# A mixture-of-experts kernel: second tiles of 32 rows, an unsplit first product for the pairs, and low parts on VectorE alone

## The chip, the cores and the metric

The kernel runs on one core of one Trainium2 chip. The metric is the device time of one execution in microseconds. TensorE (PE in the profile) multiplies matrices, VectorE (DVE), ScalarE (ACT) and GpSimd (POOL) work element by element, and SyncE (SP) issues transfers. Each engine takes its instructions in the order of its own queue.

## The reference

Three stages stand one behind the other, all in float32.

- Attention: q, k and v of shape (4, 8, 576, 64), with a causal window of 32 positions for half of the heads and a window of 128 with every fourth position for the others. Its output is a table x of 2304 rows by 512.
- Layer 1: of the rows with `x @ w_skip > 0`, each goes to the one of 8 experts with the largest `x @ w_gate`:

```python
h = np.maximum(xc[mask] @ w1[e], 0.0)
y[mask] = gate_w[mask, None] * (h @ w2[e])
```

  with w1 of 512 x 1024 and w2 of 1024 x 512; the result is added to x. Other rows stay as they are.
- Layer 2: each row goes to the two best of 8 other experts by noisy logits, and the two results are added up with their softmax weights.

With the inputs of the runs the experts of layer 1 get 199, 144, 133, 121, 112, 88, 82 and 66 rows; each expert of layer 2 gets 549 to 591.

## The kernel before, in words

**Stages.** Attention runs until about 131 us, layer 1 until about 308, layer 2 until 750, and the last results are scattered to memory by 766.7.

**Layer 1** sorts its experts by their number of rows: rank 0 has the most. It has 11 tiles of up to 128 rows, t = 0 to 10. Ranks 0, 1 and 2 have two tiles each, the others one; the order of ranks is 0, 3, 1, 4, 5, 2, 6, 7. What a tile can't hold would be worked off in a loop at the end, whose number of passes is counted from the data (`much`, L1471) and is 0 here.

A plain tile (`ExpertTile`) has its rows gathered by an indirect transfer, transposed on TensorE (op `x:t` of the list `steps`), multiplied by w1 (`h0:t` and `h1:t`, 16 matmuls of 128 x 128 each at L746, fp32, which the trace records as 32), sent through a ReLU on ScalarE (`ht`, L749), multiplied by w2 (`p0:t` and `p1:t`, L755, 4 fp32 matmuls of 512 columns each, 8 records) and closed on VectorE (`finish`: `xg`, L1355). The second tiles of ranks 1 and 2 aren't handled alone: tiles 3 and 4, and 7 and 8, are pairs (`ExpertPair`), which share each weight. A pair works with numbers split into two parts: ScalarE rounds a number to a high part (`whi`, `xg`, `xh`; `split`, L433), VectorE or GpSimd subtracts it from the number for the low part (`wlo`, `xl`; L434), and `mm3` (L439 to L441) multiplies high by high, low by high and high by low: three matmuls in the fast form for one fp32 matmul. The first product has eight steps `H0` to `H7` of 256 columns with two banks in PSUM; each bank comes free when VectorE has made `xl` (L788) from it. The second product (`P:3` for the first tile, `P:4` for the second) has 24 matmuls of 512 columns per tile.

**Weights.** An expert's weights are four pieces of 1 MB, two of w1 and two of w2 (class `Pieces`). A slot has two halves, `whi` and `wlo`, of 1 MB each. An unsplit piece is loaded into a half as it is; a piece to be split is loaded into one of three `wraw` buffers and cut into a whole slot by four `whi` on ScalarE and four `wlo`. There are five slots in turn, so a slot is filled again when the work on the fifth before it is done. In layer 1 the pairs' four pieces per rank are split, which makes 20 slots; in layer 2 all pieces are split. `every1` and `every2` say which of the low parts go to GpSimd: one in 8 for the pairs, and one in 2, 4 or 8, or all, by expert in layer 2.

**Order.** TensorE's order is written out by hand: the list `steps` for layer 1, loops for layer 2 (`hidden2` with four PSUM banks, `product2`). The orders of the other engines are made by a scheduler from dependencies and priorities. SyncE issues the weights (L482), the rows written back (L1357) and the zeros for the output (`zt`, L1360) in one queue. Between the expert steps, TensorE and VectorE make layer 2's routing: `r`, `l`, `m` make logits (`x2T`, `lgs`; L1193, L1208, L1213), `X` and `Y` steps fill tables with one-hot products (`eqf`, `onehot`, `bvf`, L358 to L388).

Of the kernel before, what the change touches and what calls it, by code (L numbers as in the profile page):

```python
# [8 lines left out]
F32 = mybir.dt.float32  # L9
# [421 lines left out]
def split(nc, hi, lo, src, eng=None):  # L431
# [12 lines left out]
class Pieces:  # L444
# [24 lines left out]
    def load(self, n):  # L469
        while self.loaded < min(n, len(self.keys), self.known):  # L470
            key = self.keys[self.loaded]
            src, every = self.src[key]
            if every is None:
# [49 lines left out]
def tile_attention_moe_moe(ctx, tc, q, k, v, w_skip, w_gate, w1, w2, v_gate, v_noise, noise, u1, u2, out):  # L523
# [17 lines left out]
    ORDER = [c for r in (0, 3, 1, 4, 5, 2, 6, 7) for c in ([K1 + r, r] if r < K1 else [K1 + r])]  # L541
    LAST = 2
# [154 lines left out]

    every1 = {1: 8, 2: 8}
    every2 = [2, 2, 8, 2, 2, 4, 2, 1]
    P = Pieces(tc, raw_p)  # L700
    for kk, src in order:
        P.plan(kk, src, every1.get(kk[1]))
    for e in range(E):
        for i in range(4):

            P.plan((2, e, i), lambda e=e, i=i: piece(u1, u2, e, i, f"o ({'p k' if e > 1 else 'k p'}) f -> p (o k) f"), every2[e])
# [58 lines left out]
    class ExpertPair:  # L765


        def __init__(self, xp):
            x = [xp.tile([128, 2, 256], F32R, name="xg2", bufs=4) for _ in range(4)]
            self.x = x[:2], x[2:]  # L770
            self.h = [xp.tile([128, KC, CAP], F32R, name=n).rearrange("p c t -> p (c t)")[:, :2048].rearrange(
                "p (f t) -> p f t", f=8) for n in ("xh2", "xl2")]

        def rows_T(self, xg, i):
            ps = bank("tp")
            for c in range(KC):
                nc.tensor.transpose(ps[:, 128 * c:128 * c + 128], xg[:, 128 * c:128 * c + 128], ident)
# [397 lines left out]
    static1 = rt.tile([128, E], F32, name="static1")  # L1175
    static2 = rt.tile([128, E], F32, name="static2")
# [45 lines left out]
    with ExitStack() as lctx:  # L1222
# [78 lines left out]
        with ExitStack() as ectx:  # L1301
# [90 lines left out]
            for op, *t in steps:  # L1392
# [70 lines left out]
        def rest_of():  # L1463
# [4 lines left out]
            nc.vector.tensor_scalar(static1, rank1, float(K1), 1.0, op0=ALU.is_lt, op1=ALU.add)  # L1468
            n1 = ro.beyond(wk, cnt1, static1, "1")[1]
# [105 lines left out]
    with tc.If(rest > 0), ExitStack() as ectx:  # L1575
# [34 lines left out]
        xcol1, xe1 = ro.extras(ep, ro.beyond(ep, cnt1, static1, "4"), static1, JR, "4")  # L1610
        rest1 = nc.values_load(much[0:1, 0:1], min_val=0, max_val=JR)
        with tc.For_i(0, rest1, 1) as i:
# [4 lines left out]
            nc.vector.tensor_add(sv[:, 1:2], sv[:, 1:2], so[:, 4:5])  # L1617
            gi = ep.tile([128, 1], I32, name="gir")
# [85 lines left out]
```

## Time and profile before

| | |
|---|---|
| median of 3 runs | 768.95 us (767.02, 768.95, 769.21) |
| profiled execution | 768.6 us, its span 766.7 us |
| TensorE busy | 734.3 us, 96% |
| weight loads of TensorE | 626.3 us, 82% |
| VectorE busy | 379.8 us, 50% |
| ScalarE busy | 309.2 us, 40% |
| GpSimd busy | 245.9 us, 32% |
| low parts on VectorE | 100 operations, 80.8 us |
| low parts on GpSimd | 60 operations, 86.5 us |
| high parts on ScalarE | 160 operations, 91.2 us |

The shares are means over stages that differ: a share of 96% says that TensorE sets the pace over most of the span, and not where the other 4% are. For that the span is read stage by stage, and each hole of TensorE is followed to what ended it. A record of a matmul lasts longer than the distance to the next one, since matmuls are pipelined; for sums the distance counts.

### The profile page before, as it was taken

To read this page: it belongs to the slowest core of one execution; us is meant where nothing else is said; L and a number is where in the kernel's file an instruction comes from. 1 tells how busy PE (TensorE), PEld (TensorE's weight loads), DVE (VectorE), ACT (ScalarE), POOL (GpSimd) and SP (SyncE) were. 2 spreads that over 40 slices of the span, in tenths; PEclk is the share of its full clock that TensorE was granted. 3 is DMA by queue.
4 is the path that set the end of the run, shared out by engine and by line. 5 is a ranking of instruction groups with operands and counts; after the bars stand their busy time and mean duration, and the time that the engine had idled before them with its cause. 6 is when DMAs were issued, how large, how long until landed. Compare 5 with 4: busy or idle time off the path is not lost.

```text
span 766.7 us, 14489 instructions
## 1 busy us (share of the span) xinstructions
PE 734.3 (96%) x5448; PEld 626.3 (82%) x5448; DVE 379.8 (50%) x1253; ACT 309.2 (40%) x824; POOL 245.9 (32%) x239
## 2 busy tenths in 40 slices
PE   8999989979999999899999999999999999999994
PEld 6877767757977887789898997997988988988883
DVE  7766866818217538934344353452552562250110
ACT  5987852124116244224442442533433334333110
POOL 4322220200033043155533533624515325445011
PEclk9999999998999999999999999999999999999997
DMA  7989565597869998243888818729529537223112
GB/s 191 175 185 244 130 210 194 192 331 247 293 219 338 336 316 296 73 110 118 218 277 212 236 69 211 203 74 233 174 85 248 155 109 146 87 40 51 15 25 30
DMA packets 129980, 136.06 MB, mean 177 GB/s; under 512 B 44784, under 2 KB 82416, under 8 KB 129904
## 3 DMA queue, kind: packets, MB, share of 16 engines
q1 hardware_dynamic: 118784, 110.90, 46.4%
q0 software_dynamic: 9808, 22.86, 14.8%
q10 hardware_dynamic: 1312, 1.31, 0.5%
q8 instruction: 45, 0.74, 0.4%
q14 instruction: 31, 0.25, 0.1%
HBM read 103.97 MB, written 31.06 MB: 176 GB/s over the span
## 4 chain that ended last, share of the span: by engine, by line
PE 79%; DVE 7%; DMA 6%; ACT 5%; issue 1%; POOL 1%; SPq 0%; POOLq 0%; DVEq 0%; ACTq 0%
PE pt L439 10%; PE pt L441 10%; PE pt L440 10%; PE po L441 5%; PE po L439 5%; PE po L440 5%; PE s L439 5%; PE s L440 5%; PE s L441 5%; PE s L746 5%; DMA wraw<-in_moe_w_dram 3%; ACT sm L182 3%; PE pt L755 3%; PE s L175 2%; DMA wlo<-in_moe_w_dram 2%; PE tp L146 2%
## 5 line engine op out<-in xcount | busy, mean ns | idle before, releaser
L434 DVE TENSOR_TENSOR wlo<-wraw,whi 128x512 fp32r<-128x512 f32 x100 | 80.8, 833 | 103.5 <-ACT whi L433 95.0
L434 POOL TENSOR_TENSOR wlo<-wraw,whi 128x512 fp32r<-128x512 f32 x60 | 86.5, 1517 | 133.6 <-ACT whi L433 117.1
L439 PE MATMUL pt<-whi,hh 128*128 128x512 f32 (+1 forms) x320 | 126.9, 396 | 0.0
L440 PE MATMUL pt<-wlo,hh 128*128 128x512 f32 (+1 forms) x320 | 126.1, 394 | 0.0
L441 PE MATMUL pt<-whi,hl 128*128 128x512 f32 (+1 forms) x320 | 126.0, 394 | 0.0
L433 ACT ACTIVATE whi<-wraw 128x512 fp32r<-128x512 f32 x160 | 91.2, 622 | 59.0 <-PE po L440 17.1
L716 POOL DMA_INDIRECT xg<-xs,gidx x51 | 53.0, 1040 | 157.9 <-PE tp L1192 32.6
L1216 POOL DMA_INDIRECT out_dram<-y,sidx x40 | 62.9, 1572 | 123.5 <-ACT y L1460 119.9
L441 PE MATMUL s<-xh,wlo 128*128 128x256 f32 (+1 forms) x256 | 72.5, 283 | 0.0
L441 PE MATMUL po<-xh,wlo 128*128 128x352 f32 x224 | 72.5, 324 | 0.0
L440 PE MATMUL s<-xl,whi 128*128 128x256 f32 (+1 forms) x256 | 72.4, 283 | 0.0
L439 PE MATMUL po<-xh,whi 128*128 128x352 f32 x224 | 72.4, 323 | 0.0
L439 PE MATMUL s<-xh,whi 128*128 128x256 f32 (+1 forms) x256 | 72.4, 283 | 0.0
L440 PE MATMUL po<-xl,whi 128*128 128x352 f32 x224 | 72.2, 322 | 0.0
L441 PEld LDWEIGHTS pt<-whi,hl 128*128 128x128 f32 (+1 forms) x320 | 58.4, 183 | 15.7
L440 PEld LDWEIGHTS pt<-wlo,hh 128*128 128x128 f32 (+1 forms) x320 | 58.4, 183 | 15.0
L439 PEld LDWEIGHTS pt<-whi,hh 128*128 128x128 f32 (+1 forms) x320 | 58.4, 182 | 14.7
L1445 DVE SCALAR_TENSOR_TENSOR hl<-po,hh 128x352 fp32r<-128x352 f32 x56 | 29.2, 522 | 69.8 <-ACT hh L1444 68.1
L1460 ACT ACTIVATE y<-pt,slots 128x512 f32<-128x512 f32 (+1 forms) x40 | 27.3, 683 | 79.6 <-PE pt L441 59.3
L182 ACT ACTIVATE sm<-sm,nmax 128x96 f32<-128x96 f32 x144 | 51.9, 362 | 16.3 <-DVE nmax L178 16.0
L1445 DVE SCALAR_TENSOR_TENSOR hl<-s,hh 128x256 fp32r<-128x256 f32 (+1 forms) x64 | 27.4, 428 | 58.1 <-ACT hh L1444 54.3
L186 POOL TENSOR_TENSOR sm<-sm,rs 128x480 f32<-128x480 f32 (+1 forms) x32 | 29.1, 911 | 75.4 <-DVE nmax L178 47.6
(409 smaller groups left out, 1459.0 us busy)
## 6 DMA issues: line engine op xcount, KB each, us to landing
wraw<-in_moe_w_dram SPq DMA_DIRECT2D x40, 1024.0 KB
whi<-in_moe_w_dram SPq DMA_DIRECT2D x12, 1024.0 KB
wlo<-in_moe_w_dram SPq DMA_DIRECT2D x12, 1024.0 KB
xq<-xg SPq DMA_DIRECT2D x24, 256.0 KB
xs<-xq SPq DMA_DIRECT2D x96, 64.0 KB
out_dram<-zt SPq DMA_DIRECT2D x46, 128.0 KB
xs<-xr SPq DMA_DIRECT2D x13, 256.0 KB
v<-in_v_dram SPq DMA_DIRECT2D x7, 432.0 KB
```

Of the source, the lines that this page charges most:

```text
L182: nc.scalar.activation(sm[:, n, :], sm[:, n, :], AF.Exp, bias=nmax[:, n:n + 1], scale=-1.0, accum_out=ssum[:, n:n + 1])
L186: nc.gpsimd.tensor_tensor(out=sm[:, n0:n1, :], in0=sm[:, n0:n1, :], in1=rs[:, n0:n1, None].to_broadcast([128, n1 - n0, 96]), op=ALU.mult)
L433: nc.scalar.activation(hi, src, AF.Copy)
L434: (eng or nc.vector).tensor_tensor(out=lo, in0=src, in1=hi.bitcast(F32), op=ALU.subtract)
L439: nc.tensor.matmul(out, lhsT=a[0], rhs=b[0], start=start, stop=False)
L440: nc.tensor.matmul(out, lhsT=a[0], rhs=b[1], start=False, stop=False)
L441: nc.tensor.matmul(out, lhsT=a[1], rhs=b[0], start=False, stop=stop)
L716: gather.last = nc.gpsimd.indirect_dma_start(out=xg, out_offset=None, in_=xs[:n, :], in_offset=bass.IndirectOffsetOnAxis(ap=idx, axis=0))
L746: nc.tensor.matmul(ph[:, 128 * f:128 * f + 128], lhsT=w[:, c, 128 * f:128 * f + 128], rhs=self.x[:, c], start=c == 0, stop=c == KC - 1)
L1216: s = nc.gpsimd.indirect_dma_start(out=out, out_offset=bass.IndirectOffsetOnAxis(ap=idx, axis=0), in_=y, in_offset=None, compute_op=ALU.add)
L1445: d = nc.vector.scalar_tensor_tensor(hl[1][:, f, s_], in0=ph, scalar=0.0, in1=hl[0][:, f, s_].bitcast(F32), op0=ALU.max, op1=ALU.subtract)
L1460: nc.scalar.activation(y[:n], py, AF.Copy, scale=slots2[:n, 2, j:j + 1])
```

## The change

The second tiles of ranks 1 and 2 now hold 32 rows (`PART`, `rows1`), and places for rows beyond are masked (`rko`, `rkr`). A pair's first product takes w1 unsplit, in plain fp32, over 128 + 32 = 160 columns: 4 matmuls for each `H` step. Its x isn't split any more; ScalarE only copies it. The hidden values are still split, and the second product is still `mm3`, with 32 columns of stationary rows for the second tile. Ranks 1 and 2 so have two pieces to be loaded into halves and two to be cut, and layer 1 uses 18 slots. All low parts are made on VectorE, in both layers. Rows that a tile of 32 can't hold go to the loop at the end (`over1`, `part1`, `done1`), which may have up to 20 passes instead of 16.

```diff
 def split(nc, hi, lo, src):

     nc.scalar.activation(hi, src, AF.Copy)
-    (eng or nc.vector).tensor_tensor(out=lo, in0=src, in1=hi.bitcast(F32), op=ALU.subtract)
+    nc.vector.tensor_tensor(out=lo, in0=src, in1=hi.bitcast(F32), op=ALU.subtract)
...
+    PART = [128, 32, 32, 128, 128, 128, 128, 128]
+    rows1 = [PART[r] if c < K1 or r >= K1 else 128 for c, r in enumerate(RANK)]
...
-            eng = self.nc.gpsimd if j % self.src[key][1] == self.src[key][1] - 1 else self.nc.vector
-            split(self.nc, hi[:, j], lo[:, j], self.raw[key][:, j], eng)
+            split(self.nc, hi[:, j], lo[:, j], self.raw[key][:, j])
...
+    rkr = cp.tile([128, T1], F32, name="rkr")
     for c, r in enumerate(RANK):
-        nc.gpsimd.memset(rko[:, c:c + 1], float(r))
+        nc.gpsimd.memset(rko[:, c:c + 1], float(r + 1))
+        nc.gpsimd.memset(rkr[:, c:c + 1], float(rows1[c]))
+    nc.vector.tensor_tensor(out=rkr, in0=ro.pidx.to_broadcast([128, T1]), in1=rkr, op=ALU.is_lt)
+    nc.vector.tensor_mul(rko, rko, rkr)
+    nc.vector.tensor_scalar(rko, rko, -1.0, None, op0=ALU.add)
...
-    every1 = {1: 8, 2: 8}
-    every2 = [2, 2, 8, 2, 2, 4, 2, 1]
+    cut1 = (1, 2)
     P = Pieces(tc, raw_p)
     for kk, src in order:
-        P.plan(kk, src, every1.get(kk[1]))
+        P.plan(kk, src, kk[1] in cut1 and kk[2] > 1)
...
     class ExpertPair:
-        def __init__(self, xp):
-            x = [xp.tile([128, 2, 256], F32R, name="xg2", bufs=4) for _ in range(4)]
-            self.x = x[:2], x[2:]
...
+        def __init__(self, xp, n):
+            self.n, m = (128, n), 128 + n
+            self.x = [xp.tile([128, 2, 256], F32, name="xg2", bufs=4)[:, :, :m] for _ in range(2)]
...
             for h in range(2):
-                split(nc, *[x[h][:, :, 128 * i:128 * i + 128] for x in self.x], ps[:, h])
+                nc.scalar.activation(self.x[h][:, :, 128 * i:128 * i + n], ps[:, h, :, :n], AF.Copy)
...
-            ph = bank("s")[:, :256]
+            ph = bank("s")[:, :sum(self.n)]
             fs = slice(128 * (f % 4), 128 * (f % 4) + 128)
             for c in range(KC):
-                mm3(nc, ph, (w[0][:, c, fs], w[1][:, c, fs]), [x[c // 2][:, c % 2] for x in self.x], c == 0, c == KC - 1)
+                nc.tensor.matmul(ph, lhsT=w[:, c, fs], rhs=self.x[c // 2][:, c % 2], start=c == 0, stop=c == KC - 1)
...
         def product(self, i, w):
-            py = bank("pt")
+            n = self.n[i]
+            py = bank("pt")[:n]
             for f in range(8):
                 wf = w(f // 4)
-                mm3(nc, py, [h[:, f, 128 * i:128 * i + 128] for h in self.h], (wf[0][:, f % 4], wf[1][:, f % 4]),
+                mm3(nc, py, [h[:, f, 128 * i:128 * i + n] for h in self.h], (wf[0][:, f % 4], wf[1][:, f % 4]),
                     f == 0, f == 7)
...
-    JR, J2 = 16, 48
+    JR, J2 = 20, 48
...
-            nc.vector.tensor_scalar(static1, rank1, float(K1), 1.0, op0=ALU.is_lt, op1=ALU.add)
-            n1 = ro.beyond(wk, cnt1, static1, "1")[1]
+            for to, by in ((static1, [(r < K1) + n // 128 for r, n in enumerate(PART)]), (part1, [n % 128 for n in PART])):
+                nc.vector.memset(to, float(by[0]))
+                for r in range(1, E):
+                    if by[r] != by[r - 1]:
+                        nc.vector.tensor_scalar(over1, rank1, float(r), float(by[r] - by[r - 1]), op0=ALU.is_ge, op1=ALU.mult)
+                        nc.vector.tensor_add(to, to, over1)
+            nc.vector.scalar_tensor_tensor(over1, in0=static1, scalar=128.0, in1=part1, op0=ALU.mult, op1=ALU.add)
+            nc.vector.tensor_tensor(out=over1, in0=over1, in1=cnt1, op=ALU.is_lt)
+            nc.vector.tensor_mul(over1, over1, cnt1)
+            n1 = ro.beyond(wk, over1, static1, "1")[1]
```

On ScalarE, around the end of tile 2's first half (`ht` of the tile in `h0:2`, `lgs` of tile 0's logits), the queue stands before so; `whi` x4 is the cut of a quarter of a piece four times, and `xg` the copies of the pair's transposed rows:

```order
104 L1208 ACTIVATE x2T<-po_2977 128x128
105 L433 ACTIVATE whi<-wraw 128x512 x4
106 L749 ACTIVATE ht_2965<-s 128x512
107 L1213 ACTIVATE lgs<-po_3041 128x16
108 L433 ACTIVATE whi<-wraw 128x512
109 L433 ACTIVATE xg_3073<-tp 128x2x128
110 L433 ACTIVATE whi<-wraw 128x512 x3
111 L433 ACTIVATE xg_3074<-tp 128x2x128
112 L749 ACTIVATE ht_2965<-s 128x512
113 L433 ACTIVATE xg_3073<-tp 128x2x128
114 L1193 ACTIVATE x2T<-tp 128x512
```

and after:

```order
104 L1215 ACTIVATE x2T<-po_2994 128x128
105 L753 ACTIVATE ht_2982<-s 128x512
106 L1220 ACTIVATE lgs<-po_3043 128x16
107 L784 ACTIVATE xg_3075<-tp 128x2x128
108 L784 ACTIVATE xg_3076<-tp 128x2x128
109 L753 ACTIVATE ht_2982<-s 128x512
110 L784 ACTIVATE xg_3075<-tp 128x2x32
111 L784 ACTIVATE xg_3076<-tp 128x2x32
112 L1200 ACTIVATE x2T<-tp 128x512
113 L433 ACTIVATE whi<-wraw 128x512 x4
114 L1215 ACTIVATE x2T<-po_3159 128x128
115 L433 ACTIVATE whi<-wraw 128x512 x4
116 L791 ACTIVATE xh_3077<-s 128x160 x3
```

The eight `whi` around `ht` and `lgs` are no longer there, and of the sixteen for rank 1 the eight for w2 stand ahead of the first `xh`.

On VectorE, ahead of the first `xl` of the pair (`L1355`, after `L1362`, closes tile 2), the queue before:

```order
700 L370 TENSOR_SCALAR onehot<-r_rowsb,ent_lo 128x128
701 L434 TENSOR_TENSOR wlo<-wraw,whi 128x512 x4
702 L362 TENSOR_TENSOR bvf<-eqf,ent_val 128x600
703 L370 TENSOR_SCALAR onehot<-r_rowsb,ent_lo 128x128 x2
704 L358 TENSOR_TENSOR eqf<-pat_2739,ent_col 128x120 x2
705 L314 COPY ohsy<-nextx 128x8
706 L434 TENSOR_TENSOR wlo<-wraw,whi 128x512 x4
707 L1355 SCALAR_TENSOR_TENSOR xg_2793<-pt,slots_2713,xg_2793 128x512
708 L788 SCALAR_TENSOR_TENSOR xl_3078<-s,xh_3077 128x256 x5
```

and after:

```order
707 L358 TENSOR_TENSOR eqf<-pat_2754,ent_col 128x120
708 L1330 TENSOR_TENSOR nextx<-cx,cntx 128x8
709 L358 TENSOR_TENSOR eqf<-pat_2754,ent_col 128x120
710 L314 COPY ohsy<-nextx 128x8
711 L434 TENSOR_TENSOR wlo<-wraw,whi 128x512 x8
712 L1362 SCALAR_TENSOR_TENSOR xg_2810<-pt,slots_2728,xg_2810 128x512
713 L792 SCALAR_TENSOR_TENSOR xl_3078<-s,xh_3077 128x160 x5
```

Two cuts of four stand among the table steps before; now eight stand in one row, right ahead of `xg` and `xl`.

On TensorE, where the pair's first product begins (`H0`), before:

```order
503 L755 MATMUL pt<-wlo,ht_2965 128x512 x4
504 L439 MATMUL s<-xg_3073,whi 128x256
505 L440 MATMUL s<-xg_3075,whi 128x256
506 L441 MATMUL s<-xg_3073,wlo 128x256
507 L439 MATMUL s<-xg_3073,whi 128x256
508 L440 MATMUL s<-xg_3075,whi 128x256
509 L441 MATMUL s<-xg_3073,wlo 128x256
510 L439 MATMUL s<-xg_3074,whi 128x256
```

and after, twelve matmuls of 256 columns have become four of 160:

```order
503 L759 MATMUL pt<-wlo,ht_2982 128x512 x4
504 L790 MATMUL s<-xg_3075,whi 128x160 x2
505 L790 MATMUL s<-xg_3076,whi 128x160 x2
506 L790 MATMUL s<-xg_3075,whi 128x160 x2
507 L790 MATMUL s<-xg_3076,whi 128x160 x2
508 L790 MATMUL s<-xg_3075,whi 128x160 x2
509 L790 MATMUL s<-xg_3076,whi 128x160 x2
```

The names without a split carry `whi` because an unsplit piece lies in a half of a slot.

## Rows read from the trace of the kernel before

**Rows 1.** Windows: start:end, length, busy PE, PEld, DVE, ACT, POOL; clock, DMA share, GB/s

```profile
170.00:180.00 10.00, 7.68 (x47) 7.31 (x47) 8.18 (x27) 5.51 (x14) 0.00 (x0) 0.66 0.95 323
310.00:320.00 10.00, 9.45 (x82) 8.86 (x80) 10.00 (x37) 3.13 (x9) 1.74 (x1) 1.00 0.07 27
320.00:330.00 10.00, 8.22 (x54) 6.66 (x53) 7.91 (x49) 1.28 (x4) 0.00 (x0) 1.00 0.35 107
400.00:500.00 100.00, 100.00 (x559) 88.14 (x558) 45.80 (x66) 40.47 (x79) 44.41 (x35) 1.00 0.68 184
```

**Rows 2.** TensorE's waits, 120 to 330 us: us in total, times, longest

```profile
PE po L324 <- ACT lgs L1213: 4.9, 1, 4.9
PE s L439 <- DVE xl L788: 2.0, 2, 1.1
PE po L324 <- DVE rest0z L382: 1.7, 1, 1.7
```

**Rows 3.** The chain that ended last, 155 to 192 us: start, us, what

```profile
161.30 8.14 DMA wraw<-in_moe_w_dram
...
171.70 0.48 ACT ht L749
...
172.32 0.28 PE po L324
...
187.98 2.50 DVE wlo L434 x4
...
191.53 0.39 PE s L439
```

**Rows 4.** TensorE's instructions in order of time, 160 to 263 us: start, us

```profile
163.58 3.73 PE L746 MATMUL s<-xt,whi 128*128 128x128 f32 x32
...
173.78 5.64 PE L746 MATMUL s<-xt,wlo 128*128 128x128 f32 x32
...
180.21 3.60 PE L755 MATMUL pt<-whi,ht 128*128 128x512 f32 x8
...
187.75 0.28 PE L440 MATMUL s<-xg,whi 128*128 128x256 f32 x1
187.87 0.28 PE L441 MATMUL s<-xg,wlo 128*128 128x256 f32 x1
...
201.94 0.40 PE L439 MATMUL pt<-whi,xh 128*128 128x512 f32 x1
...
261.86 0.41 PE L439 MATMUL pt<-whi,xh 128*128 128x512 f32 x1
```

**Rows 5.** ScalarE's instructions in order of time, 161 to 250 us

```profile
169.51 2.19 ACT L433 ACTIVATE whi<-wraw 128x512 fp32r<-128x512 f32 x4 [8.99 <-DMA wraw<-in_moe_w_dram]
...
184.46 2.18 ACT L433 ACTIVATE whi<-wraw 128x512 fp32r<-128x512 f32 x4
...
247.27 2.20 ACT L433 ACTIVATE whi<-wraw 128x512 fp32r<-128x512 f32 x4 [1.07 <-DMA wraw<-in_moe_w_dram]
```

**Rows 6.** SyncE's queue in order of time, 140 to 310 us

```profile
164.96 7.49 SPq L1360 DMA_DIRECT2D out_dram<-zt  x7
172.73 1.05 SPq L482 DMA_DIRECT2D wraw<-in_moe_w_dram  x2
...
237.86 1.36 SPq L482 DMA_DIRECT2D wraw<-in_moe_w_dram  x2
```

**Rows 7.** VectorE's instructions in order of time, 275 to 325 us

```profile
293.05 1.24 DVE L300 SCALAR_TENSOR_TENSOR iycx<-ent_idle,ixax 128x9 f32<-128x9 f32 x1
...
296.72 0.17 DVE L300 SCALAR_TENSOR_TENSOR iydx<-ent_idle,ixbx 128x9 f32<-128x9 f32 x1
```

**Rows 8.** VectorE's groups by form, 340 to 745 us: busy, mean ns, idle

```profile
L434 DVE TENSOR_TENSOR wlo<-wraw,whi 128x512 fp32r<-128x512 f32 x58 | 51.7, 908 | 85.4 <-ACT whi L433 77.9 <-ACT y L1460 4.2 <-issue 1.6
L1445 DVE SCALAR_TENSOR_TENSOR hl<-po,hh 128x352 fp32r<-128x352 f32 x56 | 29.2, 522 | 69.8 <-ACT hh L1444 68.1 <-issue 1.6
```

**Rows 9.** The page's costliest groups, GpSimd's low parts

```profile
L434 POOL TENSOR_TENSOR wlo<-wraw,whi 128x512 fp32r<-128x512 f32 x60 | 86.5, 1517 | 133.6 <-ACT whi L433 117.1
```

More of the change, by code (lines that the diff above doesn't have):

```diff
@@ L428, in extras, with split @@
         return cols, ei
-def split(nc, hi, lo, src, eng=None):
+def split(nc, hi, lo, src):
     nc.scalar.activation(hi, src, AF.Copy)
-    (eng or nc.vector).tensor_tensor(out=lo, in0=src, in1=hi.bitcast(F32), op=ALU.subtract)
+    nc.vector.tensor_tensor(out=lo, in0=src, in1=hi.bitcast(F32), op=ALU.subtract)
 def mm3(nc, out, a, b, start, stop):
@@ L454, in __init__, with plan @@
         self.known = 4
-    def plan(self, key, src, every):
-        if every is not None:
+    def plan(self, key, src, cut):
+        if cut:
             self.split.append(len(self.keys))
         self.keys.append(key)
-        self.src[key] = (src, every)
+        self.src[key] = (src, cut)
     def slot(self):
@@ L471, in load @@
             key = self.keys[self.loaded]
-            src, every = self.src[key]
-            if every is None:
+            src, cut = self.src[key]
+            if not cut:
                 if not self.half:
@@ L726, in tile_attention_moe_moe, with __init__ @@
     class ExpertTile:
-        def __init__(self, pool, xg):
-            self.pool, self.xg = pool, xg
+        def __init__(self, pool, xg, n=128):
+            self.pool, self.xg, self.n = pool, xg, n
         def rows_T(self):
-            self.x = self.pool.tile([128, KC, 128], F32, name="xt1")
-            self.h = self.pool.tile([128, 8, 128], F32, name="ht1")
+            n = self.n
+            self.x = self.pool.tile([128, KC, 128], F32, name="xt1")[:, :, :n]
+            self.h = self.pool.tile([128, 8, 128], F32, name="ht1")[:, :, :n]
             ps = bank("tp")
             for c in range(KC):
-                nc.tensor.transpose(ps[:, 128 * c:128 * c + 128], self.xg[:, 128 * c:128 * c + 128], ident)
-            nc.scalar.activation(self.x, ps.rearrange("p (c t) -> p c t", c=KC), AF.Copy)
+                nc.tensor.transpose(ps[:, 128 * c:128 * c + n], self.xg[:n, 128 * c:128 * c + 128], ident[:n, :n])
+            nc.scalar.activation(self.x, ps.rearrange("p (c t) -> p c t", c=KC)[:, :, :n], AF.Copy)
         def hidden(self, g, w, f0=0, f1=4):
@@ L1175, in tile_attention_moe_moe @@
     static1 = rt.tile([128, E], F32, name="static1")
+    part1 = rt.tile([128, E], F32, name="part1")
+    over1 = rt.tile([128, E], F32, name="over1")
     static2 = rt.tile([128, E], F32, name="static2")
@@ L1346, in start @@
                     xg = (h1[0], ep, wk, ep)[t % 4].tile([128, DM], F32, name="xg1", bufs=1 + t % 2)
-                    X[t] = ExpertTile((h1[0], ep)[t % 2], gather(xg, gidx1[:, c:c + 1], N))
+                    X[t] = ExpertTile((h1[0], ep)[t % 2], gather(xg, gidx1[:, c:c + 1], N), rows1[c])
                     with tc.issue_after(gather.last.ins):
@@ L1352, in finish @@
             def finish(t):
-                c, x = ORDER[t], X[t]
+                c, x, n = ORDER[t], X[t], X[t].n
                 x.x2 = x.xg
-                nc.vector.scalar_tensor_tensor(x.x2, in0=x.py, scalar=slots[:, 1, c:c + 1] if t else val0[:, 2:3],
-                                               in1=x.xg, op0=ALU.mult, op1=ALU.add)
+                nc.vector.scalar_tensor_tensor(x.x2[:n], in0=x.py, scalar=slots[:n, 1, c:c + 1] if t else val0[:, 2:3],
+                                               in1=x.xg[:n], op0=ALU.mult, op1=ALU.add)
                 d = nc.sync.dma_start(xs[N + 128 * c:N + 128 * c + 128, :], x.x2)
@@ L1400, in tile_attention_moe_moe @@
                     if t in PAIRS:
-                        pair[t] = pair[t + 1] = ExpertPair(xp)
+                        pair[t] = pair[t + 1] = ExpertPair(xp, X[t + 1].n)
                     if t in pair:
@@ L1609, in tile_attention_moe_moe @@
         nc.vector.tensor_copy(ent_val[:, :, :NT, 5:7], ent_val[:, :, :NT, 0:2])
-        xcol1, xe1 = ro.extras(ep, ro.beyond(ep, cnt1, static1, "4"), static1, JR, "4")
+        xcol1, xe1 = ro.extras(ep, ro.beyond(ep, over1, static1, "4"), static1, JR, "4")
+        oe = ep.tile([128, JR, E], F32, name="oe1")
+        ef1 = ep.tile([128, JR], F32, name="ef1")
+        done1 = ep.tile([128, JR], F32, name="done1")
+        nc.vector.tensor_copy(ef1, xe1)
+        nc.vector.tensor_tensor(out=oe, in0=ef1[:, :, None].to_broadcast([128, JR, E]),
+                                in1=ro.eidx[:, None, :].to_broadcast([128, JR, E]), op=ALU.is_equal)
+        first = ep.tile([128, E], F32, name="first1")
+        nc.vector.scalar_tensor_tensor(first, in0=ro.eidx, scalar=32.0, in1=static1, op0=ALU.mult, op1=ALU.add)
+        oe2 = ep.tile([128, JR, E], F32, name="oe2")
+        nc.vector.tensor_mul(oe2, oe, first[:, None, :].to_broadcast([128, JR, E]))
+        nc.vector.tensor_reduce(out=ef1, in_=oe2, axis=AX.X, op=ALU.add)
+        nc.vector.tensor_tensor(out=ef1, in0=ef1, in1=xcol1, op=ALU.is_equal)
+        nc.vector.tensor_mul(oe, oe, part1[:, None, :].to_broadcast([128, JR, E]))
+        nc.vector.tensor_reduce(out=done1, in_=oe, axis=AX.X, op=ALU.add)
+        nc.vector.tensor_mul(done1, done1, ef1)
+        nc.vector.tensor_tensor(out=done1, in0=done1, in1=ro.pidx.to_broadcast([128, JR]), op=ALU.is_le)
         rest1 = nc.values_load(much[0:1, 0:1], min_val=0, max_val=JR)
```

17 lines of the change are left out of this document (9 added, 8 removed).

## The prediction

> **What bounds the kernel now.** I read the table of windows first, for TensorE's share in each stage. In 400–500 us, the middle of layer 2, TensorE is busy 100.00 of 100 us at granted clock 1.00, VectorE only 45.80 [rows 1]: nothing taken off another engine can shorten that stretch. In layer 1 the same table has holes: 170–180 us has 7.68 busy of 10 at a granted clock of 0.66, 320–330 has 8.22, and 310–320 has 9.45 beside a VectorE that is busy 10.00 of 10. The list of waits says what ends the holes [rows 2]: one wait of 4.9 us for ScalarE's `lgs`, two waits of together 2.0 us for VectorE's `xl`, one of 1.7 us for `rest0z`. The chain of waits explains the first [rows 3]: a raw weight transfer takes 8.14 us from 161.30, ScalarE then makes four `whi`, and only behind them, in its queue's order, come `ht` (171.70) and `lgs`, which TensorE waits for until 172.32. The list of ScalarE's instructions has the same [rows 5]: `whi` x4 began at 169.51 after 8.99 us of idling for `wraw`. So the long hole is a queue held by a transfer, not work.
>
> **The change, part by part.** Sums are against the profiled execution, 768.6 us (span 766.7), which lies 0.35 below the median of 768.95.
>
> (a) The wait at 167 us. With rank 1's w1 unsplit there is no cut to make before the pair's w2 pieces, so the eight `whi` in front of and behind `ht` and `lgs` are gone (first order excerpt). `h0:2` ends at about 167.3 (3.73 us from 163.58 [rows 4]); `ht` and `lgs` then follow at once; in the chain TensorE goes on 0.62 after `ht` began (171.70 to 172.32 [rows 3]), and with what `ht` itself waits for I put that near 168.1 instead of 172.3: 4.2 us. The granted clock fell after this hole: `h1:2` has 32 records in 5.64 us from 173.78 where the same form at 163.58 has 3.73 [rows 4], and the transposes ahead of it lost about half a microsecond too. With an idle of 0.75 in place of 4.88 I take the clock to stay: 2.4 us. Bounds for that term: 0 (the clock falls all the same) to 2.6. The last product of tile 2 then ends near 180.6 instead of 187.2.
>
> (b) The pair's first product. Before, each of the 8 `f` takes 12 matmuls of 256 columns, spaced 0.118 (187.75 to 187.87 [rows 4]): 1.41 us. After, 4 fp32 matmuls of 160 columns, two records each in this trace. No row has 160 columns. From the two fp32 forms, after subtracting the 0.16 by which a record outlasts its spacing: 128 columns (3.73 − 0.16)/32 = 0.112, 512 columns (3.60 − 0.16)/8 = 0.43 a record; on the line between them 0.138, so 8 x 0.138 = 1.10 us. Bounds: 0.112 (as 128 columns) to 0.16 (somewhat above the line, as 12 records of the old form by time) a record, 0.90 to 1.28 us. Saved 0.31 per `f`, 2.5 a pair. Transposes of 32 rows save some 0.25 a pair. The second product keeps its 24 matmuls of 512 columns for either tile: nothing.
>
> (c) The wait ahead of `H2`. It stays, in another place. Only the split of rank 1's two w2 pieces is left, and ScalarE has these eight `whi` ahead of the first `xh` (first excerpt), VectorE the eight `wlo` and tile 2's closing `xg` ahead of `xl` (second excerpt); the bank of `H0` comes free with `xl`, and `H2` waits for it. The two raws are issued from 172.73, behind the seven zero transfers that hold SP for 7.49 us [rows 6]; 2 MB at the 323 GB/s of 170–180 us [rows 1] are 6.5 us, so I take them to land near 178 and 181. Then `whi` x4 2.19 [rows 5] to 183.3, the last `wlo` 0.62 (2.50 for four), and 1.05 for `xg` and `xl`, as from 190.48 to 191.53 [rows 3]: `H2` at about 185.1. `H0` and `H1` end at 182.8, so TensorE idles some 2.4 us; before, `H2` stood at 191.5. Gain so far 6.4, rounded to 6.3 for the handing over between engines. Ends: 182.8 (no wait) and 188.5 (raw as late as the `whi` of 184.46 [rows 5], plus the same chain).
> From `H2` to `P:3` before: 201.94 − 191.53 = 10.4, of which 6 x 1.41 matmuls and 1.9 other work; after 6 x 1.10 + 1.9 = 8.5. `P:3` at 193.7: gain 8.2.
>
> (d) The second pair. Before, its raws waited in SP until 237.86 [rows 6], the last `whi` x4 began at 247.27 on a transfer [rows 5], and `H2` waited 1.1 us (second of the two waits in [rows 2]). After, 18 in place of 20 slots are used, w1 needs no cut, and rank 2's w2 pieces take slots that are free two tiles earlier: no transfer is late. Gone: 1.1 wait, 2.5 matmuls, 0.25 transposes. Late next is VectorE's table steps (`bvf`, `onehot`), about 8 us in a stretch of 9 to 10: I take 0.5 back. `P:7` before at 261.86 [rows 4]; gain there 8.2 + 3.85 − 0.5 = 11.5.
>
> (e) The low parts on VectorE. 60 operations leave GpSimd (1517 ns each [rows 9]); VectorE gets them and loses 16 in layer 1, net 44, nearly all of the 60 in layer 2. Price in layer 2: TensorE and its weight loads have no wait there, VectorE is 46% busy [rows 1] and would be some 55%; `hl` at 522 ns [rows 8] has to follow TensorE through four banks, a slack of several microseconds against a burst of four `wlo` (2.5). I take 0; ends 0 and 60 x 0.62 = 37 us, if every one stood in front of an `hl` that TensorE waits for. In the transition (275–325 us) VectorE gets 4 to 10 more `wlo` at 0.62, and loses what GpSimd costs it now: `iycx` took 1.24 beside a GpSimd `wlo`, its like 0.17 alone [rows 7]; I reckon with four or five such excesses of 0.5 to 1.1, about 4 us. Net −2 to +2: I take 0.
> The Trainium skill, "SBUF — State Buffer", section "Who interferes with whom", has a rule for this: a VectorE instruction with two SBUF inputs contends with a GpSimd one that reads SBUF, and the later one blocks wholly. The 1.24 against 0.17 agrees with it.
>
> (f) Small work. Eleven more operations of about 0.17 us [rows 7] stand on VectorE near the first gather; and TensorE, busy with the first rank's tiles, has no wait there that I would lengthen. 0 to 1.9, taken as 0.5 with the memsets at the start.
>
> Sum: 768.6 − 11.5 + 0.5 = 757.6 us.
>
> **The rivals.**
> 1. *The wait only moves to `H2`.* Raws land as late as the `whi` of 184.46 suggests, `H2` at 188.5 and 3.3 of (c) lost: 760.9. For it: SP's queue is unchanged up to these raws. Against it: ScalarE began that `whi` behind another wait, not on the transfer.
> 2. *VectorE becomes the bound of the transition.* It is already at 10.00 of 10 in 310–320 [rows 1]; ten `wlo` more at 0.62, with no contention returned, cost up to 6: 757.6 + 4 to 6 = 762 to 764. Against it: VectorE waits for long stretches before 310.
> The Trainium skill speaks against the change here: "Perfetto Trace Analysis", section "Optimizing Scalar/DVE Operations", holds that work of a saturated VectorE may well be moved to ScalarE or even GpSimd, though between VectorE and GpSimd, which share a port, it might not help. By its first half this rival is right, by its second half my zero; the full 10.00 us agrees with the first, the 1.24 with the second.
> 3. *Slower.* In layer 2 VectorE's one queue holds `hl` behind a `wlo` that waits for its `whi`, and so for a slot or a transfer; on GpSimd that wait hurt nobody. VectorE's `wlo` wait 77.9 us for `whi` in this stretch already [rows 8], hidden. The mechanism decides once a single hold exceeds what the four banks cover, about 5 us; with 1.5 us exposed at each of the 8 x 2 hidden halves it is 24 us, 781. Break-even is at 11 us in all. Against it: the present waits cost TensorE nothing, so they stand in places where no `hl` is due.
> 4. *Only TensorE's own work counts.* Holes at 167 and 191 stay in another form, and 2 x 2.75 us of matmuls and transposes are all: 763.6.
>
> A change that does not do what it says: ranks 1 and 2 have 144 and 133 rows, so 128 + 32 hold them and the loop for the rest runs no pass. I give that no chance.
>
> **How the numbers follow.** Forecast 0.58; rival 1 0.12; rival 2 0.12; rival 4 0.10; rival 3 0.08. A difference under 0.3% (2.3 us: 766.6 to 771.3) can't be told from none here. Faster: all of the forecast and of rivals 1 and 2, and 0.06 of rival 4, whose 763.6 lies 3 us below the bound: 0.88. The same: the other 0.04 of rival 4 and 0.02 of rival 3, near its break-even: 0.06. Slower: the other 0.06 of rival 3. Lowest: no wait at `H2` (−2.4), 0.9 us per `f` (−3.2) or 2 from the transition: 752. Highest: rivals 2 and 4 with a microsecond of small work: 764.5.
>
> **What would show it.** In the profile after: no wait for `lgs` over 1 us near 167 and clock 1.00 in 170–180 (a); 4 fp32 matmuls in 1.10 us (b); a wait of about 2.4 us for `xl` near 183 and `P:3` near 194 (c); `P:7` near 250 (d); TensorE 100 of 100 in 400–700 (e). The forecast is wrong if TensorE shows waits for `hl` in layer 2, or if the 10 us gained by `P:7` are not there at the end.

## The result, and the profile after

The changed kernel takes 760.21 us, the median of 4 runs (758.75 to 761.13), against 768.71 us for the kernel before, timed with it (767.02 to 769.21). The ratio is 0.990, with a 95% interval from 0.9863 to 0.9937. The profiled execution took 760.57 us with a span of 758.8, 7.9 us less than before. The forecast was 757.6, its range 752 to 764.5.

The windows of the changed kernel (start:end, length, busy us of PE, PEld, DVE, ACT, POOL, then granted clock, DMA share and GB/s) answer to [rows 1]:

```profile
170.00:180.00 10.00, 10.00 (x64) 6.74 (x62) 5.97 (x32) 2.57 (x7) 0.95 (x1) 1.00 0.90 312
180.00:190.00 10.00, 7.13 (x43) 5.70 (x42) 6.45 (x12) 4.92 (x14) 0.00 (x0) 1.00 1.05 390
300.00:310.00 10.00, 9.38 (x80) 8.95 (x78) 9.85 (x42) 3.38 (x11) 0.00 (x0) 1.00 0.02 6
310.00:320.00 10.00, 8.22 (x47) 6.90 (x47) 6.99 (x39) 0.77 (x2) 0.00 (x0) 0.83 0.29 105
400.00:700.00 300.00, 300.00 (x1692) 265.91 (x1691) 136.09 (x223) 114.44 (x224) 67.56 (x48) 1.00 0.56 146
```

The stretch 170–180 us, which had 7.68 busy us at a clock of 0.66, is full at 1.00. A new hole stands in 180–190. In 300–320 TensorE's holes and VectorE's full load are those of before, some 10 us earlier, with a lower clock behind them. Layer 2 is at 300 of 300 us.

The list of TensorE's waits (us in total, times, longest), against [rows 2]:

```profile
PE s L790 <- DVE xl L792: 2.9, 1, 2.9
PE po L324 <- DVE ohsz L1134: 2.3, 1, 2.3
PE po L324 <- ACT lgs L1220: 0.6, 1, 0.6
PE tp L726 <- DMA xg<-xs,gidx: 0.5, 1, 0.5
```

The wait for `lgs` has gone from 4.9 to 0.6 us. In place of two short waits for `xl` there is one of 2.9, and the wait in the transition has 2.3 where it had 1.7 and 0.5 in a second one.

TensorE's instructions in order of time (start, us, what), against [rows 4]; the names of lines have moved by a few (L750 is L746, L790 the pair's first product):

```profile
164.67 3.73 PE L750 MATMUL s<-xt,whi 128*128 128x128 f32 x32
...
169.18 0.23 PE L324 MATMUL po<-ohsx,r_tri 128*128 128x144 bf16 x1 [0.65 <-ACT lgs L1220]
...
170.06 3.74 PE L750 MATMUL s<-xt,wlo 128*128 128x128 f32 x32
...
182.01 2.34 PE L790 MATMUL s<-xg,whi 128*128 128x160 f32 x16
187.22 1.35 PE L790 MATMUL s<-xg,whi 128*128 128x160 f32 x8 [2.87 <-DVE xl L792]
...
195.64 0.51 PE L439 MATMUL pt<-whi,xh 128*128 128x512 f32 x1
```

The second `L750` takes 3.74 us, as the first does, where [rows 4] had 5.64. The row of 16 records is `H0` and `H1`, and `H2` at 187.22 carries the wait. `P:7` starts so:

```profile
251.51 0.51 PE L439 MATMUL pt<-whi,xh 128*128 128x512 f32 x1
```

ScalarE's list, against [rows 5], shows `lgs` with nothing of a cut ahead of it, and the two cuts for w2, each begun on the landing of its transfer:

```profile
168.94 0.19 ACT L1220 ACTIVATE lgs<-po 128x16 f32<-128x16 f32 x1
...
179.52 2.19 ACT L433 ACTIVATE whi<-wraw 128x512 fp32r<-128x512 f32 x4 [4.07 <-DMA wraw<-in_moe_w_dram]
...
183.05 2.19 ACT L433 ACTIVATE whi<-wraw 128x512 fp32r<-128x512 f32 x4 [1.18 <-DMA wraw<-in_moe_w_dram]
```

The same two transfers leave SyncE behind seven zero transfers, as in [rows 6]:

```profile
166.05 7.23 SPq L1367 DMA_DIRECT2D out_dram<-zt  x7
173.62 0.99 SPq L481 DMA_DIRECT2D wraw<-in_moe_w_dram  x2
```

Three places that the table below needs and that were not shown of the kernel before: `H0`, the routing of the last two tiles (`ohsz`) and that routing's last matmul.

```profile
187.23 0.68 PE L439 MATMUL s<-xg,whi 128*128 128x256 f32 x1
...
322.13 0.18 PE L324 MATMUL po<-ohsz,r_tri 128*128 128x16 bf16 x1 [1.72 <-DVE rest0z L382]
...
330.47 0.18 PE L333 MATMUL po<-cz,r_ones 128*128 128x8 bf16 x1
```

Where the 7.9 us come from, place by place, worked out from these starts (after: 311.72 and 321.48 for the last two). The last column has the prediction's terms; rounded, they add up to 11.2, where its sum has 11.0.

| from | to | before, us | after, us | gain | forecast |
|---|---|---|---|---|---|
| start | first half of tile 2 (`h0:2`) | 163.58 | 164.67 | −1.1 | −0.5 |
| `h0:2` | routing behind `lgs` | 8.74 | 4.51 | 4.2 | 4.2 |
| that | `H0` | 14.91 | 12.83 | 2.1 | 2.4 |
| `H0` | `H2` | 4.30 | 5.21 | −0.9 | −0.2 |
| `H2` | `P:3` | 10.41 | 8.42 | 2.0 | 1.9 |
| `P:3` | `P:7` | 59.92 | 55.87 | 4.0 | 3.4 |
| `P:7` | routing of the last two tiles | 60.27 | 60.21 | 0.1 | 0 |
| that | its last matmul | 8.34 | 9.76 | −1.4 | 0 |
| that | end of the span | 436.2 | 437.3 | −1.1 | 0 |

### The profile page after: what moved, and what is told of

Its sections match the earlier page's. It is cut to its first block, busy times and chain, and to the rows that moved or that the text cites. A ratio compares the mean times of both kernels' runs of the same rounds, so it can differ in the third digit from the quotient of the medians.

```text
span 758.8 us, 14282 instructions
## 1 busy us (share of the span) xinstructions
PE 728.5 (96%) x5384; PEld 616.8 (81%) x5384; DVE 378.6 (50%) x1302; ACT 299.7 (40%) x808; POOL 162.3 (21%) x190
## 4 chain that ended last, share of the span: by engine, by line
PE 86%; DVE 5%; ACT 4%; DMA 3%; issue 1%; POOL 0%; POOLq 0%; SPq 0%; ACTq 0%; DVEq 0%
PE pt L441 10%; PE pt L440 10%; PE pt L439 10%; PE s L750 6%; PE pt L759 6%; PE po L441 5%; PE po L440 5%; PE po L439 5%; PE s L441 4%; PE s L440 4%; PE s L439 4%; ACT sm L182 3%; PE s L175 3%; PE s L790 2%; PE tp L146 2%; PE pt L197 1%
## 5 line engine op out<-in xcount | busy, mean ns | idle before, releaser
L434 DVE TENSOR_TENSOR wlo<-wraw,whi 128x512 fp32r<-128x512 f32 x144 | 93.4, 685 | 116.7 <-ACT whi L433 101.9
L433 ACT ACTIVATE whi<-wraw 128x512 fp32r<-128x512 f32 x144 | 82.1, 624 | 53.0 <-DMA wraw<-in_moe_w_dram 16.2
L439 PEld LDWEIGHTS s<-xh,whi 128*128 128x128 f32 x256 | 48.7, 190 | 0.7
L440 PEld LDWEIGHTS s<-xl,whi 128*128 128x128 f32 x256 | 48.7, 190 | 0.3
```

Of the source, the lines that this page charges most:

```text
L434: nc.vector.tensor_tensor(out=lo, in0=src, in1=hi.bitcast(F32), op=ALU.subtract)
L439: nc.tensor.matmul(out, lhsT=a[0], rhs=b[0], start=start, stop=False)
L440: nc.tensor.matmul(out, lhsT=a[0], rhs=b[1], start=False, stop=False)
```

## The experiments

Each of these was timed against the kernel before on the same chip: 768.24 us for the first four, 767.35 for the last three. Every trace is of one execution.

**Low parts alone.** One part of the change in the kernel before: no low part of layer 2 on GpSimd. (An 8 in `every2` sends none there, since a piece has only four low parts; so the 8 in `every1` sent none either, and all 60 were layer 2's.)

```diff
-    every2 = [2, 2, 8, 2, 2, 4, 2, 1]
+    every2 = [8] * E
```

> The kernel before with one part of the change alone: all low parts of layer 2 on VectorE, none on GpSimd. My theory (layer 2 is set by TensorE, which has no wait there): 768.7 within 2 us, TensorE 100 of 100 us in 400-700, the hole near 320 within 1.5 us of its 2.3 us before. Rival, VectorE's queue exposes the moved work: 5 to 25 us slower, with waits of TensorE for hl in layer 2. Second rival, contention of GpSimd and VectorE was what cost the transition: 2 to 4 us faster.

768.51 us, ratio 1.001 (0.998 to 1.0039). Its waits from 120 us to the end, and its window of layer 2:

```profile
PE s L439 <- DVE xl L788: 2.5, 2, 1.6
PE po L324 <- DVE ohsz L1129: 2.4, 1, 2.4
PE po L324 <- ACT lgs L1213: 2.3, 1, 2.3
```

```profile
400.00:700.00 300.00, 300.00 (x1683) 264.94 (x1682) 139.22 (x227) 115.00 (x225) 66.43 (x48) 1.00 0.56 147
```

TensorE has no wait in layer 2, though VectorE now makes 108 `wlo` in 340–745 us instead of 58. The moved work costs nothing that can be told from the median, and gains nothing (the interval leaves room for 1.5 us faster to 3 slower): the first theory holds, both rivals fall. The list holds a second lesson: layer 1 is here that of the kernel before, yet the wait for `lgs` is 2.3 us, not 4.9. Its length hangs on when the raw piece lands, and that differs from execution to execution: the first `whi` began at 167.34 here and at 169.51 in the kernel before, though the transfer was issued later here, at 161.83 instead of 161.30. The granted clock fell behind the shorter wait too, to 0.57 in 171–175.

**128 rows.** The changed kernel, with full second tiles:

```diff
-    PART = [128, 32, 32, 128, 128, 128, 128, 128]
+    PART = [128, 128, 128, 128, 128, 128, 128, 128]
```

> The changed kernel, but with 128 rows in the second tiles of ranks 1 and 2, so the pairs' first product takes the unsplit w1 over 256 columns. My theory: the wait for lgs near 168 stays at 0.7 us and the clock at 1.00, which keeps some 6.5 us of the gain; each H step takes 8 records at about 0.22, 1.75 us against 1.09, which costs 16 x 0.66 = 10.5, less up to 1.3 that the wait ahead of H2 gets shorter: 760.2 + 9 = 769, about the time before. Rival, what counts is the wait taken away and the columns hardly at all: 762 to 764.

769.84 us, ratio 1.0025 (1.0001 to 1.005). TensorE's first product of the pair:

```profile
189.63 2.61 PE L790 MATMUL s<-xg,whi 128*128 128x256 f32 x8 [2.42 <-DVE xl L792]
...
195.97 3.62 PE L790 MATMUL s<-xg,wlo 128*128 128x256 f32 x16
```

Two `H` steps (16 records) take 3.62 us, and less the overhang of 0.16 a step is 1.73; the forecast had 1.75. The wait for `lgs` is 0.6 as in the changed kernel, and the clock stays at 1.00 behind it. But it fell behind the wait of 2.42, to 0.61 in 190–194: the 8 records of the first row are one `H` step and take 2.61. From `H2` to `P:3` are 13.9 us, where 6 x 1.73 and the 1.9 of other work make 12.3; 1.6 went to the clock in this execution, which at 772.03 us is 2.2 above its median. So the unsplit w1 by itself wins the waits and loses as much in matmuls: without the narrower tile the change would have been worth nothing.

**w1 split.** The changed kernel, with the pairs' w1 and x split as before, over 160 columns:

```diff
-        P.plan(kk, src, kk[1] in cut1 and kk[2] > 1)
+        P.plan(kk, src, kk[1] in cut1)
...
-                nc.tensor.matmul(ph, lhsT=w[:, c, fs], rhs=self.x[c // 2][:, c % 2], start=c == 0, stop=c == KC - 1)
+                mm3(nc, ph, (w[0][:, c, fs], w[1][:, c, fs]), [x[c // 2][:, c % 2] for x in self.x], c == 0, c == KC - 1)
```

> The changed kernel, but with w1 and x of the pairs split again: 12 fast matmuls of 160 columns for each H step. My theory: the wait for lgs near 168 is back at about 4 to 5 us with the lower clock behind it (some 6.5 us lost), while an H step takes 12 x 0.075 to 0.118 = 0.9 to 1.4 us against 1.09: 762 to 768. Rival, the 32 rows alone make the gain and the unsplit w1 adds nothing: 758 to 761.

768.77 us, ratio 1.0008 (0.9984 to 1.0032): slower than either theory's range had it, by 0.8 us and more. Two matmuls of the first `H` step, and the windows of the second pair:

```profile
186.52 0.28 PE L440 MATMUL s<-xg,whi 128*128 128x160 f32 x1
186.63 0.27 PE L441 MATMUL s<-xg,wlo 128*128 128x160 f32 x1
```

```profile
235.00:245.00 10.00, 9.25 (x45) 4.93 (x44) 7.31 (x20) 5.73 (x14) 5.24 (x5) 1.00 0.92 297
245.00:255.00 10.00, 8.65 (x58) 8.18 (x57) 5.98 (x15) 3.18 (x9) 0.00 (x0) 0.78 1.03 345
255.00:265.00 10.00, 10.00 (x66) 9.91 (x65) 5.17 (x18) 2.45 (x7) 0.94 (x1) 0.70 1.05 392
```

The spacing is 0.11 us, against 0.118 for 256 columns [rows 4]: 96 columns less save 6%, and an `H` step takes 1.33 instead of 1.41. So narrowing the tile gains some 1.3 us in 16 steps as long as w1 is split (an estimate from these spacings). The waits for `lgs` (2.2 us, not the 4 to 5 of my theory) and `xl` (2.3) are back. In this execution the clock also fell behind a hole of 1.35 us at 248.6, to 0.50 in 250.7–260.7, which costs some 5 us (10 us at a spacing of 0.213); the execution took 773.66 us, 4.9 above the median of the 12 runs, so it is not the rule.

The two halves of the change in layer 1 so need each other: either alone (each with all low parts on VectorE) gives about 0, together 8.

**Zeros later.** The changed kernel, with tile 1's seven zero transfers issued behind tile 2:

```diff
-            ZERO = [0, 7, 14, 17, 20, 24, 35, 39, 39, 45, 46, 46]
+            ZERO = [0, 7, 7, 17, 20, 24, 35, 39, 39, 45, 46, 46]
```

> The changed kernel with the seven zero transfers behind tile 1 issued behind tile 2 instead, so that rank 1's two raw pieces of w2 no longer stand behind them in SyncE's queue. My theory (the wait of 2.9 us ahead of H2 comes from the raws' late landing): the wait is under 0.6 us, P:3 starts 2.3 to 2.9 us earlier, and the end is 757.5 to 758.5. Rival, the time is given back later in layer 1 or in the transition, because the zeros or VectorE's steps hold the second pair: P:3 earlier, but 759.5 to 761 in all.

757.17 us, ratio 0.9858 (0.9822 to 0.9894). SyncE's queue and the start of `P:3`:

```profile
165.22 0.34 SPq L1364 DMA_DIRECT2D xs<-xg  x1
165.76 1.44 SPq L481 DMA_DIRECT2D wraw<-in_moe_w_dram  x2
```

```profile
192.09 0.50 PE L439 MATMUL pt<-whi,xh 128*128 128x512 f32 x1
```

The raws leave at 165.8 instead of 173.6, and TensorE has no wait for `xl` at all. Counted from the last matmul of layer 1's first routing (134.24 here, 135.25 in the changed kernel), `P:3` comes 2.5 us sooner; from `P:3` to the end it is 562.8 here and 563.2 there. The time is kept, as the theory had it (the median is 0.3 below its range). The interval overlaps that of the changed kernel, so it is the trace that shows the 2.5 us.

**GpSimd kept.** The changed kernel, with the 60 low parts of layer 2 on GpSimd (the old `every2` and `split`).

```diff
+    every2 = [2, 2, 8, 2, 2, 4, 2, 1]
...
```

> The changed kernel, but with the 60 low parts of layer 2 on GpSimd as before. My theory (where they are made does not matter): within 1.5 us of the changed kernel's 760.2, the hole near 312 us between 1.7 and 2.4 us. Rival, VectorE's moved work made the hole and the lower clock behind it that cost the changed kernel some 2 us after the second pair: 757 to 758.5, hole under 1.2 us. Other rival, contention with GpSimd costs more than the moved work: 762 to 764.

760.2 us, ratio 0.9897 (0.985 to 0.9944), the changed kernel's ratio. Its waits, 120 to 330 us:

```profile
PE s L792 <- DVE xl L794: 3.6, 1, 3.6
PE po L324 <- DVE rest0z L382: 1.6, 1, 1.6
PE po L324 <- ACT lgs L1222: 0.6, 1, 0.6
PE po L388 <- DVE onehot L370: 0.5, 1, 0.5
```

The hole in the transition is 1.6 us and 0.5 in a second wait, together about what it is with all low parts on VectorE, and the clock fell behind it here too (0.80 in 310–315). From `P:7` to the routing's last matmul are 70.1 us here and 70.0 in the changed kernel. So the moved work did not make the hole, nor the lower clock. (The clock also fell behind the 3.6 us ahead of `H2`, to 0.59 in 186–190, which it didn't in the changed kernel.)

**Without the code for the rest.** The changed kernel without the mask on `rko` and all of `over1`, `part1` and `done1`; the code for rows that a tile of 32 can't hold is left out.

```diff
-            for to, by in ((static1, [(r < K1) + n // 128 for r, n in enumerate(PART)]), (part1, [n % 128 for n in PART])):
...
+            nc.vector.tensor_scalar(static1, rank1, float(K1), 1.0, op0=ALU.is_lt, op1=ALU.add)
...
```

> The changed kernel without what it adds for rows that a tile of 32 can't hold: the mask at the start, the eleven small operations near the first gather and the code ahead of the loop are left out (no row needs them with these inputs). My theory: the first tile's steps start 0.7 us earlier and the first gathered rows' transposes 1.1 us earlier, so 759.0 to 759.6. Rival, none of it is on the path: 760.2 within 0.4; the 1.1 us later start then comes from something else.

761.11 us, ratio 0.9916 (0.9883 to 0.995): not faster, and 0.5 above the rival's range too. The last matmul of layer 1's first routing starts at 135.4 here, at 135.3 in the changed kernel, at 132.4 in the execution of "GpSimd kept", which has all that code, at 134.6 in the kernel before and at 136.7 in that of "128 rows". My expectation fell: the later start isn't shown to come from the change, and it differs between executions by up to 4 us.

**Zeros later, and the routing of the last tiles two steps later.** On top of "zeros later":

```diff
-                  (0, 5): [RZ.place, TY.step],
+                  (0, 7): [RZ.place, TY.step],
```

> Like zeros_later, and the routing step of the last two tiles (place of z, with its matmuls at L324) stands behind the last step of expert 0's first hidden half instead of two steps earlier, so that TensorE has two steps of real work while VectorE gets there. My theory (TensorE waits 2.3 us for VectorE's routing at that place, and then loses about 1.3 us to the lower clock): the hole shrinks below 1 us, the clock stays at 1.00, and 2 to 3.5 us are gained on zeros_later's 757.2: 753.7 to 755.2. Rival, the wait only moves to the next step, since VectorE's queue is full there and the hidden steps' banks wait for hl: within 0.7 us of zeros_later.

752.06 us, ratio 0.980 (0.9756 to 0.9844), clear of the changed kernel's interval. TensorE around that routing, and two windows:

```profile
306.09 0.18 PE L324 MATMUL po<-ohsz,r_tri 128*128 128x16 bf16 x1
...
309.61 0.46 PE L388 MATMUL po<-bvf,onehot 128*128 128x280 bf16 x2 [0.46 <-DVE bvf L362]
```

```profile
300.00:305.00 5.00, 5.00 (x44) 4.91 (x43) 4.92 (x28) 1.50 (x5) 0.00 (x0) 1.00 0.00 0
305.00:310.00 5.00, 4.49 (x29) 3.40 (x28) 4.87 (x33) 0.63 (x2) 0.00 (x0) 1.00 0.59 183
```

(A step of the table, `TY.step`, moves along with the routing.) The routing's first matmul finds its input there; of the 2.3 us one wait of 0.46 is left, and the clock stays at 1.00. From `P:7` to that routing's last matmul are 66.9 us here, 69.7 in "zeros later": 2.8 us, within what was expected. The median is 5.1 us lower, 1.6 below the expected range. In the two profiled executions the last matmul of layer 1's first routing starts 1.9 us earlier here (132.38 against 134.24); that such an earlier start is the rest of the medians' difference too isn't shown. This version beats both kernels.

## Why the prediction was right, and where it was off

**(a) The wait at 167 us** was sized to a tenth: 4.2 us and 2.1 of 2.4 for the clock. But that it agrees so closely is in part luck, since both come from one execution of the kernel before. "Low parts alone" and "w1 split", where the cut of rank 1's w1 also stands ahead of `lgs`, show that wait at 2.3 and 2.2 us. From `h0:2` to `H0` they take 20.2 and 20.1 us, the kernel before 23.7 and the changed kernel 17.3: by those two executions the unsplit w1 gains 2.8 us there, by the profile before 6.3. Which of them is usual isn't shown. The execution of "low parts alone" took 766.19 us, 2.3 below the median of its 12 runs, and the profiled one of the kernel before lay 0.35 below its median; the medians of the two kernels differ by 8.5 us, the profiled executions by 8.0.

**(b) The matmuls.** A record of 160 columns takes (2.34 − 0.16)/16 = 0.136 us, 0.138 was interpolated; 1.09 us a step, 1.10 forecast. The second product did not change.

**(c) The wait ahead of `H2`** came in the place and by the chain that the prediction gave: raws behind the zeros, `whi`, eight `wlo`, `xg`, `xl`. Its size was 2.9, not 2.4: the second raw landed at 183.05, two microseconds later than I took it, of which 0.9 is its later issue (173.62, where I reckoned with 172.73). "Zeros later" took the wait away by the queue alone, which shows the cause. The measured 760.21 lies nearer to rival 1's 760.9 than to the forecast, but not by rival 1's mechanism: that had `H2` at 188.5 behind a wait of 5.7 us (from 182.8). `H2` came at 187.22 because `H0` itself stood at 182.01 instead of 180.6, and from `H0` to `H2` only 0.7 us more went than forecast.

**(d) The second pair** gained 4.0 instead of 3.4: the 0.5 that I gave back to VectorE's table steps was not taken.

**(e) The low parts** show no wait of TensorE in 340–745 us, as forecast, and rival 3 is gone: `wlo` has 108 operations there at a mean of 685 ns against 908 in [rows 8]. So VectorE's load hardly grew: 136.09 us of 400–700, or 45%, where I had 55% and the kernel before has 131.28:

```profile
400.00:700.00 300.00, 300.00 (x1679) 264.66 (x1678) 131.28 (x185) 116.44 (x228) 123.84 (x91) 1.00 0.57 150
```

The longer `wlo` come with GpSimd's share: "GpSimd kept" has 928 ns, "low parts alone" 684. The line of the changed kernel:

```profile
L434 DVE TENSOR_TENSOR wlo<-wraw,whi 128x512 fp32r<-128x512 f32 x108 | 70.0, 685 | 94.4 <-ACT whi L433 89.1 <-issue 2.8 <-DMA xs<-xq 1.6
```

In the transition `iycx`, which took 1.24 us beside a GpSimd `wlo` [rows 7], takes 0.16:

```profile
281.01 0.16 DVE L300 SCALAR_TENSOR_TENSOR iycx<-ent_idle,ixax 128x9 f32<-128x9 f32 x1
```

So the contention was real, as the Trainium skill has it ("SBUF — State Buffer", "Who interferes with whom"). Its end pays for the added `wlo` from `P:7` to the routing of the last two tiles: VectorE makes 20 of them there instead of 10 and is busy for the same time, before and after:

```profile
261.86:322.13 60.27, 58.00 (x381) 46.08 (x380) 40.92 (x140) 21.68 (x51) 17.62 (x12) 1.00 0.69 241
251.51:311.72 60.21, 57.87 (x381) 44.55 (x381) 40.90 (x152) 22.26 (x51) 1.94 (x2) 1.00 0.67 238
```

The net of zero was right up to there. Rival 2's mechanism is there, VectorE at 9.85 of 10 in 300–310, but the hole is about what it is with GpSimd's share kept (2.3 against 1.6 and 0.5).

**The step that was mis-sized** is the end of (e): for the transition the sum has 0, with ends of 2 us either way, and no term for the clock. The prediction had named it as a sign of being wrong that the gain by `P:7` is not there at the end; `P:7` came 10.35 us sooner, the end 7.9. So 2.5 us went in between, and in that the account fell short, though the time is within its range. The wait for `ohsz` was followed by a clock of half speed:

```profile
311.72 0.18 PE L324 MATMUL po<-ohsz,r_tri 128*128 128x16 bf16 x1 [2.34 <-DVE ohsz L1134]
...
313.50 0.41 PE L439 MATMUL s<-xh,whi 128*128 128x256 f32 x1
...
314.14 0.41 PE L439 MATMUL s<-xh,whi 128*128 128x256 f32 x1
```

Matmuls of 256 columns stand 0.215 us apart, where [rows 4] has 0.118; that is the lower level, 1.2 GHz, and lasted 2.5 us, some 1.2 of them lost; the table has 1.4 for the stretch. In the kernel before the same hole, 1.7 us behind one of 0.55, had no such tail. Nor had "low parts alone" and "128 rows" behind the same hole of 2.4 and 2.3 us: from that routing to its last matmul they take 8.3 us as the kernel before does, where the changed kernel takes 9.8. "GpSimd kept" has the lower clock, so the 1.4 us can't be put down to the moved work. It fell in five of the six traces of the changed kernel and its variants that have this hole, and in neither of the two others; whether the change has a part in it or an execution's chance, isn't shown.

Up to the transposes of the next gathered rows, which wait 0.45 for their transfer, 0.65 more went. Here the moved work does seem to cost a little. GpSimd issues the first of these gathers, before and after:

```profile
331.26 0.96 POOL L716 DMA_INDIRECT xg<-xs,gidx  x1 [19.52 <-DVE bcnt L1466]
323.13 0.94 POOL L719 DMA_INDIRECT xg<-xs,gidx  x1 [49.61 <-DVE xt L399]
```

That is 0.8 us behind the routing's last matmul before, and 1.65 after, though VectorE's operations in between take the same time. In "GpSimd kept" it is 0.8 as well, in the six other traces, all with no low parts on GpSimd, 1.3 to 1.65; the transposes come 4.3 us behind that matmul in the two with GpSimd's share and 4.6 to 5.1 in the rest. Why GpSimd starts later after its long idling isn't shown. The remaining 0.4 I have not followed. The 0.6 that the start came later than forecast is spread between executions, by "without the code for the rest".

Rival 4, that only TensorE's own work counts, falls with the second row of the table, and with "128 rows": there the `H` steps cost 16 x 0.32 = 5.1 us more than before, and the median is only 1.6 longer (0.1 to 3.8 by the interval). The rest, some 3 us, is waits that went.

## What to carry to other kernels

A wait may be removed by taking work out of the queue ahead of it, but look at once for what stands ahead of the next wait: here the next raws of the same queue held `H2`, and a line that changes the order of issue gave 2.5 us more. Before counting on narrower tiles, find what sets the spacing of the matmuls: with a new weight for every split matmul, 160 columns instead of 256 saved 6% here, and four unsplit matmuls of 160 columns in place of twelve of 256 saved 0.32 us of 1.41. Size a wait from more than one execution: the one at 167 us was 4.9 us in the profile and 2.2 to 2.3 in two other traces with the same cause. And a gain in front of a stage that ends in another engine's hole arrived there whole (60.27 and 60.21 us from `P:7` to the hole), but the clock behind the hole differs from run to run; give it a term in the sum.

## What the runs showed of the hardware

The spacing of fast fp32 matmuls with a new weight of 128 columns each hardly moves with the moving columns at these widths: 0.111 us for 160 columns, 0.118 for 256 (0.113 in the last two `H` steps of the first pair before). The Trainium skill, "TensorE: Matmul & The Clock Gate", section "LDWEIGHTS (loading the stationary operand)", has the load's time go with the columns of the stationary operand. The 0.111 fits that, but no run here varies the stationary columns at these widths. A record of unsplit fp32 goes with the moving columns: 0.112, 0.136, 0.216 and 0.43 us for 128, 160, 256 and 512.

VectorE's `wlo`, which reads two operands, takes longer when GpSimd makes some of the low parts: the mean of `wlo` in 340–745 us was 908 ns before, 928 in "GpSimd kept", and 685 and 684 in the changed kernel and "low parts alone".

The clock did not follow the length of a hole. The granted clock behind holes of TensorE:

| hole ahead of | trace | hole, us | granted clock behind it |
|---|---|---|---|
| routing behind `lgs` | "low parts alone" | 2.27 | 0.57 in 171–175 |
| `H2` | "128 rows" | 2.42 | 0.61 in 190–194 |
| `H2` | changed kernel | 2.87 | 1.00 |
| `H2` | "without the code for the rest" | 3.29 | 1.00 |
| `H2` | "GpSimd kept" | 3.63 | 0.59 in 186–190 |
| routing of the last two tiles | changed kernel | 2.34 | 0.52 in 311.7–315.2 |
| routing of the last two tiles | "low parts alone" | 2.36 | 1.00 |
| routing of the last two tiles | "128 rows" | 2.33 | 1.00 |
| routing of the last two tiles | "GpSimd kept" | 1.62 | 0.63 in 312–316 |
| `H2` of the second pair | "w1 split" | 1.35 | 0.50 in 250.7–260.7 |

The same hole at the same place, 2.3 to 2.4 us, is followed by either level in different traces. What decides it is not settled by these runs.
